# One dense step moved within each cycle of attention scores: from ahead of the last score to ahead of the third

## The chip, the cores and the metric

The kernel runs on one core of one Trainium2 chip. The metric is the device time of one execution in microseconds (us), lower is better. A core has five engines that work side by side: TensorE (PE in the profile; its weight loads are shown apart as PEld), VectorE (DVE), ScalarE (ACT), GpSimd (POOL) and SyncE (SP), which here issues most of the DMA transfers. PE writes its products to PSUM, a memory of eight banks, and ACT or DVE take them out.

## The reference

One transformer block over 2048 tokens of width 512, in f32: layer norm, attention with 32 heads of width 16 that share one key and one value head, residual, layer norm, gated feed-forward with a GELU gate and an inner width of 1792, residual.

```
def _A_ref(x, wq, wk, wv, wo):
    q = (x @ wq).reshape(B, S, H, Dh).transpose(0, 2, 1, 3)
    k = x @ wk
    v = x @ wv
    scores = jnp.einsum("bhqd,bkd->bhqk", q, k) * (Dh ** -0.5)
    p = _softmax(scores, axis=-1)
    o = jnp.einsum("bhqk,bkd->bhqd", p, v)
    return o.transpose(0, 2, 1, 3).reshape(B, S, H * Dh) @ wo

def _B_ref(x, w_gate, w_up, w_down):
    return (_gelu(x @ w_gate) * (x @ w_up)) @ w_down

x = A_x
h = x + _A_ref(_layernorm(x, axis=-1), A_wq, A_wk, A_wv, A_wo)
h2 = h + _B_ref(_layernorm(h, axis=-1), B_w_gate, B_w_up, B_w_down)
```

## The kernel before

**Attention.** The 2048 queries are cut into 4 blocks of 512, the 32 heads into 8 groups of 4, and the 2048 keys into 16 chunks of 128. For one block, one group and one chunk there are two *scores* in the sense of this document: `score(n)` (it calls `scores`, L368) issues two matmuls of PE side by side, for two heads, into a PSUM tile `s` of two banks, and one exponential of ACT (L372, 128 x 1024) that writes half of a tile `p`. An even and the next odd score fill one `p`. A *weighing* (`weigh`, L376) multiplies such a `p` by the values: four matmuls of 32 columns, which the profile shows as eight, into the accumulator `acc`. In the part of the program that matters there are two tiles `s`, so a score can be written only when the exponential of the score two before it has ended; there are five tiles `p`, and one `acc`, which DVE empties at the end of a group (L389).

**Dense work.** While the attention of block b runs, PE also does the dense work of block b - 1: the projection by `wo`, the layer norm's transposes, and the feed-forward. It is a generator (`dense`), and every `next` of it issues one *dense step*: two matmuls of 64 rows each, on the two halves of the array, into different banks (in `duo`, L548, and `weave`, L883). Three banks rotate among its products. A product is made in two halves: after the first half DVE marks the bank (L556, L906), and the other half of the array goes on with it at least LAG = 6 steps later; a bank is given to a new product at least 6 steps after its last one is done. DVE takes the finished products out (L744, L757 for gate and up, L825 for down), works on the GELU gate with ACT's tanh (L760), and also divides the attention's results (reciprocals, L416), for which it needs transfers by DMA.

**The order.** The order on PE, ACT, DVE, POOL and SP is written out by the program, instruction by instruction; nothing is moved by a scheduler. The 32 scores of a group and block are cut into six cycles of SIZES = (6, 5, 5, 6, 5, 5) scores, so that the cycles of a group begin with scores 0, 6, 11, 16, 22 and 27. A cycle issues its scores one by one, and after score j it issues as many dense steps as the j-th number of its `shares` says; at the end of the cycle come the weighings of all finished `p` but the newest. Which shares hold is set by the kind of the cycle: 8 cycles of a block are "long" (table LONG by the number of scores), 36 are "woven" (WOVEN, and LAST for the last cycle of a group), two are "short", one is a "gap" without dense steps of this kind, and the rest has none. In `(0, 5, 3, 3, 0)` no step follows the first score, 5 the second, 3 the third, 3 the fourth and none the fifth: the third score stands behind 5 dense steps. A step that ends a part of the dense work (CUT) ends the current share. Waiting work of DVE (`soon`, `lazy`) is taken from its list one entry for each score, so its place in DVE's order depends on where the scores stand among the steps; a product's evacuation and the load of later weights on SP (`done`, `next_w1`) stand at the step that ends it. Loads of queries (`load_q`, L353) for the next group are issued on SP at the third chunk of each group.

**Cycle names used below.** The fives that begin with scores 6 and 22 are *even fives*, the one that begins with 11 the *odd five*, the one that begins with 27 the *last five*.

Of the kernel before, what the change touches and what calls it, by code (L numbers as in the profile page):

```python
# [48 lines left out]
def kernel(  # L49
# [97 lines left out]
    def attend(first):  # L147
        with ExitStack() as outer:
            with tc.manual_schedule(
                engines={mybir.EngineType.PE, mybir.EngineType.Pool, mybir.EngineType.Activation}  # L150
            ):
                run(outer, first)


    def run(outer, first):
# [890 lines left out]
        width = 3  # L1046

        PLAIN = {5: (0,) * 5, 6: (0,) * 6}
        LONG = {5: (0, 5, 4, 3, 0), 6: (0, 5, 3, 3, 1, 0)}
        SHORT = {5: (0, 6, 3, 3, 0), 6: (0, 6, 3, 3, 0, 0)}  # L1050
        assert sum(SIZES) == 2 * KC
        assert [f for fs in RUNS for f in fs] == list(range(FC))
        assert [len(fs) for fs in RUNS] == [4] * (len(RUNS) - 1) + [2]

        WOVEN = {6: (0, 5, 3, 3, 3, 0), 5: (0, 5, 3, 3, 0)}
        LAST = (0, 5, 4, 3, 0)
        kinds = (
            ["long"] * 4 + ["gap"] + ["woven"] * 6 * len(SIZES) + ["long"] * 4 + ["short"] * 2
        )
# [5 lines left out]
        for c in range(LEAD[0], (NB - 1) * NG * len(SIZES)):  # L1065
# [10 lines left out]
            if kind == "long":  # L1076
                shares = LONG[size]
            elif kind == "woven":
                shares = LAST if cg == len(SIZES) - 1 else WOVEN[size]
            elif kind == "short":  # L1080
# [384 lines left out]
```

## Time and profile before

| | |
|---|---|
| median of 3 runs | 1422.04 us (1422.02 to 1422.42) |
| span of the profiled execution | 1421.8 us |
| PE busy | 1405.0 us, 99% |
| PEld busy | 760.5 us, 53% |
| ACT busy | 1036.2 us, 73% |
| DVE busy | 540.5 us, 38% |
| granted PE clock, mean | 0.999 |

The span runs from the first to the last instruction of one profiled execution; the times of the runs are taken without the profile. The ends of PE's matmuls are modelled and overlap the next ones, so a busy share of 99% does not tell that the matmuls follow each other without loss. The distances between starts do: they are read in the timeline, which lists instructions by start and length. A weight load row that is marked with a releaser stood waiting for it.

### The profile page before, as it was taken

The numbers are of one execution on the slowest core, as the hardware profiler recorded it, in microseconds if no ns is written. First come the engines' busy times: TensorE is split into PE (matmuls) and PEld (weight loads), VectorE is DVE, ScalarE is ACT, GpSimd is POOL, SyncE is SP. The second block draws the span as 40 slices with busy tenths as digits, with TensorE's granted clock in tenths as the row PEclk, the third lists the DMA queues.
The fourth block names the chain that finished last, engine by engine and source line by source line (L and its number), as shares of the span: only waits on it lengthen the run. The fifth ranks groups of instructions, "written<-read, shape, count | busy, mean of one in ns | idle before, by whom it ended". The sixth has DMA issues, their size and how long they took to land.

```text
span 1421.8 us, 25267 instructions
## 1 busy us (share of the span) xinstructions
PE 1405.0 (99%) x10502; PEld 760.5 (53%) x10502; DVE 540.5 (38%) x964; ACT 1036.2 (73%) x1149; POOL 229.3 (16%) x326
## 2 busy tenths in 40 slices
PE   9999999999999999999999999999999999999998
PEld 7533333225555555555555555554455555557886
DVE  7422322204352333514252432413343342427665
ACT  7699999997777787777777777877777777772000
POOL 6467776741000000000000000000000000002000
PEclk9999999999999999999999999999999999999999
DMA  4456766643242242213252332203243241434551
GB/s 158 155 187 213 228 202 220 204 162 107 82 157 82 88 143 86 88 41 113 94 168 78 100 132 84 89 23 123 92 140 116 86 145 35 140 125 137 178 207 63
DMA packets 66850, 180.31 MB, mean 127 GB/s; under 512 B 9484, under 2 KB 9484, under 8 KB 66696
## 3 DMA queue, kind: packets, MB, share of 16 engines
q1 hardware_dynamic: 56800, 144.43, 30.8%
q0 software_dynamic: 9760, 34.08, 7.4%
q8 instruction: 84, 1.38, 0.4%
q14 instruction: 38, 0.31, 0.1%
q10 hardware_dynamic: 168, 0.10, 0.0%
HBM read 130.87 MB, written 47.45 MB: 125 GB/s over the span
## 4 chain that ended last, share of the span: by engine, by line
PE 89%; ACT 6%; DVE 1%; DMA 1%; issue 1%; POOL 0%; SPq 0%; DVEq 0%; ACTq 0%; POOLq 0%
PE acc L376 31%; PE s L368 19%; PE pu L883 8%; PE pg L883 8%; ACT p L372 6%; PE pd L883 5%; PE pq L194 3%; PE pd L548 3%; PE pg L570 3%; PE pd L570 3%; PE pu L570 3%; PE pp L548 2%; PE pp L691 1%; PE pxt L623 1%; DMA w<-w_d 0%
## 5 line engine op out<-in xcount | busy, mean ns | idle before, releaser
L372 ACT ACTIVATE p<-s 128x1024 f32<-128x1024 f32 x1024 | 965.3, 1061 | 243.9 <-PE s L368 242.7
L376 PE MATMUL acc<-p,v_sb 128*32 128x512 f32 x4096 | 488.2, 598 | 0.1
L368 PE MATMUL s<-qg,kaug 50*128 50x512 f32 x1984 | 394.4, 432 | 4.1 <-ACT p L372 3.4
L368 PEld LDWEIGHTS s<-qg,kaug 50*128 50x128 f32 x1984 | 171.4, 184 | 284.3 <-ACT p L372 165.8
L376 PEld LDWEIGHTS acc<-p,v_sb 128*32 128x32 f32 x4096 | 109.4, 109 | 234.1 <-issue 225.8
L883 PE MATMUL pg<-x2h,w 64*128 64x512 f32 x672 | 211.9, 392 | 1.3 <-DMA w<-w_d 0.8
L883 PE MATMUL pu<-x2h,w 64*128 64x512 f32 x672 | 212.1, 392 | 0.0
L883 PEld LDWEIGHTS pg<-x2h,w 64*128 64x128 f32 x672 | 115.9, 186 | 14.3 <-DVE mark_pg L906 1.2
L883 PEld LDWEIGHTS pu<-x2h,w 64*128 64x128 f32 x672 | 116.0, 186 | 11.9
L883 PE MATMUL pu<-x2l,w 64*128 64x512 f32 x336 | 122.2, 391 | 0.0
L883 PE MATMUL pg<-x2l,w 64*128 64x512 f32 x336 | 122.1, 391 | 0.0
L126 POOL TENSOR_SCALAR rstd<-mv 128x1 f32<-128x1 f32 x16 | 3.5, 221 | 683.6 <-DVE mv L124 683.5
L760 ACT ACTIVATE ga<-ga 128x512 f32<-128x512 f32 x56 | 36.4, 656 | 88.7 <-DVE ga L755 88.7
L883 PE MATMUL pd<-w,gh 64*128 64x512 f32 x384 | 81.7, 391 | 0.0
L825 DVE TENSOR_TENSOR h<-h,pd 128x512 f32<-128x512 f32 x48 | 31.9, 684 | 114.7 <-PE pd L883 65.7
L389 DVE COPY oT<-acc 128x512 f32<-128x512 f32 x32 | 22.1, 691 | 138.5 <-PE acc L376 138.2
L1092 DVE SCALAR_TENSOR_TENSOR ga<-ga,g 128x512 f32<-128x512 f32 x72 | 49.7, 691 | 49.8 <-ACT ga L760 48.4
L416 DVE RECIPROCAL oc<-oc 128x128 f32<-128x128 f32 x64 | 56.3, 921 | 27.0 <-DMA oc<-acc_d 12.3
L744 DVE COPY g<-pg 128x512 f32<-128x512 f32 x56 | 38.7, 691 | 64.4 <-PE pg L883 58.7
L883 PEld LDWEIGHTS pu<-x2l,w 64*128 64x128 f32 x336 | 58.0, 186 | 6.8
L883 PEld LDWEIGHTS pg<-x2l,w 64*128 64x128 f32 x336 | 58.0, 186 | 5.2
L757 DVE TENSOR_TENSOR g<-g,pu 128x512 f32<-128x512 f32 x56 | 38.3, 683 | 40.5 <-PE pu L883 30.6
(260 smaller groups left out, 1406.3 us busy)
## 6 DMA issues: line engine op xcount, KB each, us to landing
w<-w_d SPq DMA_DIRECT2D x112, 512.0 KB
w<-w_d SPq DMA_DIRECT2D x28, 1024.0 KB
qg<-q_d SPq DMA_DIRECT2D x62, 200.0 KB
q_d<-qh SPq DMA_DIRECT2D x32, 256.0 KB
acc_d<-oT SPq DMA_DIRECT2D x31, 256.0 KB
oc<-acc_d SPq DMA_DIRECT2D x124, 64.0 KB
w_d<-w_0b POOLq DMA_DIRECT2D x14, 512.0 KB, 4.6
w_d<-w_1b POOLq DMA_DIRECT2D x14, 512.0 KB, 3.8
```

Of the source, the lines that this page charges most:

```text
L194: nc.tensor.matmul(pq, wt[:, d, c * P : (c + 1) * P], xt[:, d, :], start=(n == 0), stop=(n == 3 * DC - 1),)
L368: nc.tensor.matmul(s[:, a, :], kaug[rows, kc * P : (kc + 1) * P], qg[rows, u, :], start=True, stop=True,)
L372: nc.scalar.activation(p[:, 2 * u : 2 * u + 2, :], s, AF.Exp, scale=SCALE)
L376: nc.tensor.matmul(acc[32 * j : 32 * j + 32, :], v_sb[:, kc, :], p[:, j, :], start=(kc == 0), stop=(kc == KC - 1), skip_group_check=True,)
L416: nc.vector.reciprocal(oc[:, 1, sl], oc[:, 1, sl])
L548: nc.tensor.matmul(banks[k], lhsT[rows], rhs[rows], start=(turn == 0 and i == 0), stop=(turn == 1 and i == n - 1), skip_group_check=True,)
L570: nc.tensor.matmul(bank, lhsT, rhs, start=(i == 0), stop=(i == len(ts) - 1))
L744: nc.vector.tensor_copy(g, pg)
L757: nc.vector.tensor_tensor(g, g, pu, op=ALU.mult)
L760: nc.scalar.activation(a, a, AF.Tanh, scale=GELU_A * GELU_C)
L883: nc.tensor.matmul(e["bank"], lhsT[rows], rhs[rows], start=i == 0 and not e["both"], stop=last and e["both"], skip_group_check=True,)
L1092: (soon or lazy).pop(0)()
```

## The change

The number of dense steps in each cycle stays. In the tables LONG, WOVEN and LAST the share after the second score goes from 5 to 6, and the share ahead of the last score goes down by one (in the six-score long cycle the one ahead of the fifth score). SHORT and PLAIN stay, and so does every function.

```diff
-        LONG = {5: (0, 5, 4, 3, 0), 6: (0, 5, 3, 3, 1, 0)}
+        LONG = {5: (0, 6, 4, 2, 0), 6: (0, 6, 3, 2, 1, 0)}
         SHORT = {5: (0, 6, 3, 3, 0), 6: (0, 6, 3, 3, 0, 0)}
...
-        WOVEN = {6: (0, 5, 3, 3, 3, 0), 5: (0, 5, 3, 3, 0)}
-        LAST = (0, 5, 4, 3, 0)
+        WOVEN = {6: (0, 6, 3, 3, 2, 0), 5: (0, 6, 3, 2, 0)}
+        LAST = (0, 6, 4, 2, 0)
```

In the order of the instructions this moves, per cycle, the third score and those between it and the last one by one dense step each. On DVE a few entries of the waiting lists change places with marks and evacuations by one score. On SP, in two blocks, the two loads of queries of one group come behind one weight load instead of ahead of it. ACT's and POOL's orders stay.

## The prediction

> **What bounds the kernel now.** I read the page first, then the busy time of the stretch that the change touches, then who waits for whom in it, and last the timeline of single cycles. Columns of the stretch's row: sum, then busy time and instructions of PE, PEld, DVE, ACT and POOL, granted clock, DMA share, GB/s; of a timeline row: start, length (us), engine, line, operation, tiles, count, and in brackets the idle time before it with its releaser.
>
> ```profile
> span 1421.8 us, 25267 instructions
> PE 1405.0 (99%) x10502; PEld 760.5 (53%) x10502; DVE 540.5 (38%) x964; ACT 1036.2 (73%) x1149; POOL 229.3 (16%) x326
> 322.00:1280.00 958.00, 953.32 (x7844) 516.85 (x7848) 349.11 (x642) 731.18 (x795) 11.11 (x26) 1.00 0.31 102
> PEld s L368 <- ACT p L372: 75.9, 220, 1.2
> ACT p L372 <- PE s L368: 225.6, 147, 2.8
> ```
>
> All edited cycles lie between 322 and 1280 us. TensorE (PE) is busy for 953 of those 958 us at full granted clock, so time can only come from small hesitations inside its stream. The fourth row says where to look: the weight load (PEld) of a score stood waiting 220 times for an exponential of ScalarE (ACT). The fifth says that ACT in turn idles about once per cycle, waiting for a score. So the two engines hand over to each other within a cycle. Here is one woven cycle, five scores beginning with an even one, 3 weighings behind it:
>
> ```profile
> 496.29 0.39 PE L883 MATMUL pu<-x2l,w 64*128 64x512 f32 x1
> ...
> 496.52 0.40 PE L883 MATMUL pu<-x2h,w 64*128 64x512 f32 x1
> ...
> 496.70 0.19 PEld L368 LDWEIGHTS s<-qg,kaug 50*128 50x128 f32 x2 [0.22 <-ACT p L372]
> 496.76 0.45 PE L368 MATMUL s<-qg,kaug 50*128 50x512 f32 x2
> ...
> 497.04 0.40 PE L883 MATMUL pu<-x2h,w 64*128 64x512 f32 x1
> ...
> 498.45 0.39 PE L883 MATMUL pu<-x2h,w 64*128 64x512 f32 x1
> ...
> 498.53 0.19 PEld L368 LDWEIGHTS s<-qg,kaug 50*128 50x128 f32 x2
> ...
> 499.01 2.78 PE L376 MATMUL acc<-p,v_sb 128*32 128x512 f32 x24
> ```
>
> ACT in the same cycle, its first exponential and the third with the fourth:
>
> ```profile
> 495.62 1.03 ACT L372 ACTIVATE p<-s 128x1024 f32<-128x1024 f32 x1 [2.04 <-PE s L368]
> 497.44 1.95 ACT L372 ACTIVATE p<-s 128x1024 f32<-128x1024 f32 x2
> ```
>
> PE starts one slot (a dense step of two half-array matmuls, or a score of two) every 0.23 us: 496.29 to 496.52. There are two score buffers, so the third score needs the end of the first exponential: 495.62 + 1.03 = 496.65, and its load starts 0.05 later, at 496.70. That is 0.18 behind the start of the last dense step (496.52). The next dense step starts at 497.04, 0.52 after 496.52, where two slots take 0.46: 0.06 us are lost. So a load can be late by 0.18 - 0.06 = 0.12 us without cost; what goes beyond is paid in full. The last score's load is 0.08 late (498.53 against 498.45): free, with 0.04 to spare. ACT runs the exponentials of a cycle back to back, about 0.91 apart (495.62 to the third at 497.44).
>
> **The change, part by part.** No instruction is added or removed; the dense steps keep their order. In a cycle of kind long, woven or last, one dense step (two matmuls, 0.23 us) goes ahead of the third score and one fewer stands ahead of the last, or in the six-score long cycle ahead of the fifth. What this can win is the loss at the third score; what it can lose is lateness of a later one. With S the loss saved and d a delay of the exponential that the last score needs, the last load is late by (now) + S + d, because PE reaches it S earlier and ACT does not. A cycle therefore changes by -S + max(0, now + S + d - 0.12).
>
> The delay d is bounded so: the third score ends 0.23 later and its exponential may miss its turn. The lag from a score's end to its exponential, where ACT stands idle, is in the last cycle of a group:
>
> ```profile
> 382.20 0.39 PE L368 MATMUL s<-qg,kaug 50*128 50x512 f32 x2
> 382.70 1.03 ACT L372 ACTIVATE p<-s 128x1024 f32<-128x1024 f32 x1
> 383.62 1.02 ACT L372 ACTIVATE p<-s 128x1024 f32<-128x1024 f32 x1
> 383.46 0.64 PE L376 MATMUL acc<-p,v_sb 128*32 128x512 f32 x4
> ```
>
> Lag 382.70 - 382.59 = 0.11. The cycles, by type (each woven group of heads has two six-score cycles, two even fives, one odd five and one last five; 3 blocks of 6 groups):
>
> *Even fives, 36.* S = 0.06. The third score would end at 496.76 + 0.23 + 0.39 = 497.38, its exponential could start at 497.49 against 497.44 now: d = 0.05. Change -0.06 + (0.08 + 0.06 + 0.05 - 0.12) = +0.01, sum +0.4 us. If d were 0 it would be -0.04, sum -1.4.
>
> *Six-score cycles, 36.* The two kinds of them:
>
> ```profile
> 366.47 0.39 PE L883 MATMUL pg<-x2h,w 64*128 64x512 f32 x1
> ...
> 366.70 0.47 PE L368 MATMUL s<-qg,kaug 50*128 50x512 f32 x2
> 367.00 0.39 PE L883 MATMUL pg<-x2l,w 64*128 64x512 f32 x1
> 369.32 0.39 PE L883 MATMUL pu<-x2h,w 64*128 64x512 f32 x1
> 369.40 0.19 PEld L368 LDWEIGHTS s<-qg,kaug 50*128 50x128 f32 x2
> ```
>
> ```profile
> 387.67 0.39 PE L883 MATMUL pu<-x2l,w 64*128 64x512 f32 x1
> ...
> 387.89 0.48 PE L368 MATMUL s<-qg,kaug 50*128 50x512 f32 x2
> 388.21 0.40 PE L883 MATMUL pu<-x2h,w 64*128 64x512 f32 x1
> 388.62 1.95 ACT L372 ACTIVATE p<-s 128x1024 f32<-128x1024 f32 x2
> 390.55 0.39 PE L883 MATMUL pg<-x2l,w 64*128 64x512 f32 x1
> ...
> 390.62 0.19 PEld L368 LDWEIGHTS s<-qg,kaug 50*128 50x128 f32 x2
> ```
>
> In the first S = 367.00 - 366.47 - 0.46 = 0.07 and the last load is 0.08 late. In the second S = 388.21 - 387.67 - 0.46 = 0.08 and it is 0.07 late; the third score would end at 387.89 + 0.23 + 0.39 = 388.51, plus 0.11 is 388.62, exactly when its exponential starts now: d = 0, which I take for the first too. Changes -0.07 + 0.03 = -0.04 and -0.08 + 0.03 = -0.05, 18 each: -0.7 and -0.9 us. With d = 0.05 they are +0.01 and 0.
>
> *Odd fives, 18.* Nothing to save:
>
> ```profile
> 483.10 0.39 PE L883 MATMUL pg<-x2l,w 64*128 64x512 f32 x1
> 483.22 0.19 PEld L368 LDWEIGHTS s<-qg,kaug 50*128 50x128 f32 x2 [0.16 <-ACT p L372]
> 483.56 0.39 PE L883 MATMUL pg<-x2h,w 64*128 64x512 f32 x1
> ```
>
> The load is just 0.12 late and two slots take 0.46. I book 0.
>
> *Last fives (18) and five-score long cycles (17).* With 6, 4, 2 the fourth score comes 0.23 later and its exponential with it (ACT waits for it, as at 382.70), so the fifth ends near 383.62 + 0.23 + 1.02 = 384.9. Of the weighings behind it only the third reads it, and that starts two thirds of the 2.78 us for three (the row at 499.01), 1.8, after 383.46, at 385.3: 0.4 of cover; without it the 0.23 would be paid, 4 us in all. About five long ones begin even and save 0.05: -0.2 us.
>
> *Six-score long cycles, 7.* Their last score stands behind one dense step and waits openly for ACT already:
>
> ```profile
> 612.88 0.39 PE L548 MATMUL pd<-w,gl 64*128 64x512 f32 x2
> 613.41 0.19 PEld L368 LDWEIGHTS s<-qg,kaug 50*128 50x128 f32 x2 [0.57 <-ACT p L372]
> ```
>
> ACT's chain ends these cycles, so they save nothing and lose d, I take 0.03: +0.2 us.
>
> *VectorE and the queues.* Some DVE operations change places by one score, and in two of the three blocks one load of queries is issued behind one weight load instead of ahead of it on SP. The query loads:
>
> ```profile
> 798.44 1.77 SPq L528 DMA_DIRECT2D w<-w_d  x1
> 800.25 0.76 SPq L353 DMA_DIRECT2D qg<-q_d  x2
> ...
> 839.81 0.75 SPq L353 DMA_DIRECT2D qg<-q_d  x2
> ```
>
> They are issued a group (40 us) apart, early in one group for the next, so an exchange with an issue of 1.8 us has more than 30 us of cover; without it the next group's first score would be late by those 1.8. I book 0 for both; where DVE can bite is the third rival.
>
> **Sum**: +0.4 - 0.7 - 0.9 + 0 - 0.2 + 0.2 = -1.2 us. With d = 0 at the even fives -3.0; with d = 0.05 everywhere +0.6. The profiled execution spans 1421.8 us and would span 1420.6; the median of the runs lies 0.24 above that span, so 1420.8, between 1419.0 and 1422.6.
>
> **The rivals.** *First: the whole loss at the third score is won.* For it: no row shows a score ahead of a weighing with a load between 0.12 and 0.3 late, so the limit there is carried over from dense steps. The saving would be 36 x 0.06 + 18 x 0.07 + 18 x 0.08 + 0.2 = 5.1 us, 1416.9 us. Against: the 0.12 measured at 496.52, and a weighing needs the score's matmuls gone just as much. Beside this stands a rule of the Trainium skill (TensorE: Matmul & The Clock Gate, "Architectural detail: the array is 16× 32×32, not 1× 128×128"): a matmul can begin before its weight load completes. By that rule the lateness of the last score would be free up to its matmul; the row at 496.70, whose load was late by 0.18 and still cost 0.06, does not agree ahead of a dense step.
>
> *Second, slower: ACT runs dry and the last score pays.* If the third exponential starts 0.10 later instead of 0 to 0.05, every last load passes 0.12: even fives +0.06, sixes +0.06 and +0.05, odd fives 0.08 + 0.10 - 0.12 = +0.06 (their last load taken as late as the others'), in all 2.2 + 1.1 + 0.9 + 1.1 = 5.3 us, about 1427.3. It decides from d of some 0.04 on. For it: the third exponential already starts only 0.05 before its input would be there. Against: the lag of 0.11 is measured, and 0.10 more is not in any row.
>
> *Third: a dense bank comes free too late.* Three banks rotate among the dense products, and a run of six steps has no score inside it to give DVE time. It happens now where DVE waits for a transfer:
>
> ```profile
> DVE oc L416 <- DMA oc<-acc_d: 12.3, 7, 4.1
> 477.76 0.18 PEld L883 LDWEIGHTS pg<-x2h,w 64*128 64x128 f32 x1 [0.71 <-DVE h L825]
> ```
>
> At each of these seven places one slot less of cover costs up to 0.23, together 1.6: 1420.8 + 1.6 = 1422.4. Against: the order of the evacuations against the steps stays, and only the scores between them shift.
>
> **How the numbers follow.** The forecast has 0.62, the first rival 0.16, the second 0.12, the third 0.10. A measurement of this kernel can tell about 0.2% (2.8 us) from no change. Faster by more: the first rival and 0.02 of the forecast's tail, 0.18. Slower by more: the second rival and 0.01 of the third, 0.13. Within: 0.69. The range reaches from 1417.4, near the first rival, to 1424.4, half way into the second.
>
> **What would show it.** Right: third-score loads wait no more in the even fives and sixes (0.46 from the last step before it to the next one), last loads 0.14 to 0.19 late with the weighing 0.58 to 0.63 behind the last step instead of 0.56, cycles shorter by 0.05 at most, and the waits of scores for ACT moved and not gone. The first rival would show last loads as late with weighings still at 0.56; the second, third exponentials starting 0.10 behind their turn; the third, waits of dense loads for DVE beyond those of now. The forecast is wrong if a cycle's end moves by more than 0.06 either way.

## The result and the profile after

| | before | after |
|---|---|---|
| median of 21 runs each | 1422.04 us (1421.18 to 1423.15) | 1419.77 us (1418.94 to 1421.44) |
| span of the profiled execution | 1421.8 us | 1417.5 us |
| its own time | not measured | 1419.23 us |
| PEld of scores: idle | 284.3 us | 256.4 us |

The change makes the kernel 2.27 us faster: ratio 0.9984, with a 95% interval of 0.9977 to 0.9990, that is 1.4 to 3.3 us. That is real but below the 0.2% that the prediction set as the limit of "no change". The profiled span fell by more, 4.3 us, and a section below says why that pair shows too much.

First the head of the page of the changed kernel, then its busy time in the same stretch (columns as in the prediction), then its waits there: waiter, releaser, total, count, longest.

```profile
span 1417.5 us, 25266 instructions
PE 1401.8 (99%) x10502; PEld 786.5 (55%) x10502; DVE 542.6 (38%) x964; ACT 1041.4 (73%) x1149; POOL 228.7 (16%) x326
```

```profile
322.00:1280.00 958.00, 954.32 (x7873) 544.28 (x7874) 350.51 (x643) 738.63 (x798) 14.14 (x29) 1.00 0.30 103
```

```profile
ACT p L372 <- PE s L368: 215.7, 172, 2.8
PEld s L368 <- ACT p L372: 70.1, 157, 1.2
DVE oc L416 <- DMA oc<-acc_d: 11.3, 7, 3.4
```

PE is as "busy" as before, 954 of 958 us, and runs 29 more matmuls in the same stretch: the same work, packed closer. The waits of score loads for an exponential went from 220 with 75.9 us to 157 with 70.1 us. They have moved more than gone: 63 fewer, but the ones left are longer. A single cycle shows where. This is the even five that corresponds to the one in the prediction, from the timeline of the changed kernel (start, length, engine, line, operation, tiles, count, idle before with its releaser):

```profile
495.40 0.39 PE L883 MATMUL pg<-x2h,w 64*128 64x512 f32 x1
495.40 0.19 PEld L368 LDWEIGHTS s<-qg,kaug 50*128 50x128 f32 x2
495.63 0.39 PE L368 MATMUL s<-qg,kaug 50*128 50x512 f32 x2
...
495.87 0.39 PE L883 MATMUL pg<-x2l,w 64*128 64x512 f32 x1
...
497.03 0.39 PE L883 MATMUL pg<-x2h,w 64*128 64x512 f32 x1
497.21 0.19 PEld L368 LDWEIGHTS s<-qg,kaug 50*128 50x128 f32 x2 [0.22 <-ACT p L372]
497.25 0.46 PE L368 MATMUL s<-qg,kaug 50*128 50x512 f32 x2
497.64 0.64 PE L376 MATMUL acc<-p,v_sb 128*32 128x512 f32 x4
```

The load of the third score (495.40) starts with the last dense step before it, waits for nothing, and the next dense step follows 0.47 behind (495.40 to 495.87): before it was 0.52. The load of the last score (497.21) is now the one that waits for ACT; it is 0.18 late against the step at 497.03, and the weighing starts 0.61 behind that step (497.64). ACT runs the five exponentials without a pause, as before:

```profile
494.28 4.71 ACT L372 ACTIVATE p<-s 128x1024 f32<-128x1024 f32 x5 [1.95 <-PE s L368]
```

In the six-score cycle that answers to the second one of the prediction the last load is 0.17 late (390.55 to 390.72), and the weighing again 0.61 behind the step:

```profile
388.00 0.39 PE L883 MATMUL pg<-x2h,w 64*128 64x512 f32 x1
...
388.46 0.39 PE L883 MATMUL pu<-x2h,w 64*128 64x512 f32 x2
...
390.55 0.39 PE L883 MATMUL pg<-x2l,w 64*128 64x512 f32 x1
...
390.72 0.19 PEld L368 LDWEIGHTS s<-qg,kaug 50*128 50x128 f32 x2 [0.21 <-ACT p L372]
...
391.16 0.64 PE L376 MATMUL acc<-p,v_sb 128*32 128x512 f32 x4
```

**All cycles.** The next table takes the distance between the first scores of successive cycles, read from the starts in the two traces and grouped by the exact order of scores, steps and weighings; the medians leave the few disturbed cycles out. "Third" and "last" are the distances across that score: from the dense step ahead of it to the dense step or weighing behind it. Counts are below the plan's where a cycle is cut otherwise or a record is missing.

| cycle (number) | cycle, before to after | third | last | change x number |
|---|---|---|---|---|
| even fives (33) | 6.699 to 6.674 | 0.527 to 0.469 | 0.562 to 0.612 | -0.8 |
| odd fives (17) | 5.779 to 5.781 | 0.467 to 0.468 | 0.559 to 0.563 | 0 |
| sixes, two weighings (16) | 6.798 to 6.742 | 0.547 to 0.468 | 0.560 to 0.608 | -0.9 |
| sixes, three weighings (18) | 7.625 to 7.586 (13) and 7.594 (5) | 0.530 to 0.468 | 0.558 to 0.584 | -0.7 |
| last and long fives (27) | 6.876 to 6.862 | 0.474 to 0.468 | 0.562 to 0.565 | -0.4 |
| the same, two weighings (5) | 6.025 to 5.995 | 0.474 to 0.466 | 0.562 to 0.560 | -0.2 |
| long sixes (5) | 7.576 to 7.583 | 0.520 to 0.467 | 0.967 to 1.000 | 0 |

Added up before rounding, that is -2.8 us. The rest of the 4.3 us between the two spans is something else: single cycles in which a dense step, or a score, waited longer than in the others of their shape. Of the kernel before, from the view of waits:

```profile
PEld pg L883 <- DVE mark_pg L906: 1.2, 1, 1.2
PE pg L883 <- DMA w<-w_d: 0.8, 1, 0.8
PEld pg L883 <- DVE h L825: 0.7, 1, 0.7
PEld pg L883 <- DVE g L757: 0.7, 2, 0.5
```

The changed kernel's profile has none of these rows. Cycles longer than the median of their shape by over 0.1 us add up to 2.2 us in the profiled execution before (at 393.0, 474.3, 1016.1 and 1125.2 us) and to 0.4 after (1013.5 and 1122.3). They are called *bank waits* below, though not all of them wait for a bank. Those at 393.0 and 474.3 wait for DVE (the rows of L757 and L825). Those at 1013.5 and 1016.1 come from scores that wait for an exponential (0.28 us at the load at 1019.78 before and at 1017.28 after). The largest, 1.06 us in the cycle at 1125.2, waits for a transfer of weights; the rows of this place, before and after:

```profile
1123.14 0.37 SPq L528 DMA_DIRECT2D w<-w_d  x1
1128.59 0.16 DVE L906 COPY mark_pg<-pg 128x1 f32<-128x1 f32 x1 [1.23 <-PE pg L883]
1129.33 0.18 PEld L883 LDWEIGHTS pg<-x2h,w 64*128 64x128 f32 x1 [1.20 <-DVE mark_pg L906]
1129.36 0.46 PE L883 MATMUL pg<-x2h,w 64*128 64x512 f32 x1 [0.80 <-DMA w<-w_d]
```

```profile
1120.31 0.37 SPq L528 DMA_DIRECT2D w<-w_d  x1
1125.43 0.16 DVE L906 COPY mark_pg<-pg 128x1 f32<-128x1 f32 x1 [0.95 <-PE pg L883]
1125.48 0.18 PEld L883 LDWEIGHTS pg<-x2h,w 64*128 64x128 f32 x1 [0.30 <-issue]
```

The row at 1129.33 names DVE's mark, but the mark had ended at 1128.75, 0.58 earlier, and in the changed kernel the load starts ahead of its mark's end (1125.48 against 1125.59). What both loads follow, by 0.10 to 0.11 us, is the last of the 16 updates of the weight transfer's semaphore: at 1129.23 before, 6.1 us behind the issue, and at 1125.38 after, 5.1 us behind it. Both kernels issue this transfer 4.1 us behind the first exponential of the group, so the new order does not bring it earlier; why its last part took longer in one execution was not tested.

The profiled execution before took longer than the median of its runs (about 1423.5 us, by the link at the end of the account below) and the one after less (1419.23), so most of these 1.8 us belongs to the two executions and not to the pair. Without it the spans differ by 2.5 us, near the 2.27 of the medians; the 0.3 us between this and the sum over the cycles lies outside the table.

### The profile page after: what moved, and what is told of

It is laid out like the page before. It is cut to its first block, busy times and chain, and to the rows that moved or that the text cites. A ratio compares the mean times of both kernels' runs of the same rounds, so it can differ in the third digit from the quotient of the medians.

```text
span 1417.5 us, 25266 instructions
## 1 busy us (share of the span) xinstructions
PE 1401.8 (99%) x10502; PEld 786.5 (55%) x10502; DVE 542.6 (38%) x964; ACT 1041.4 (73%) x1149; POOL 228.7 (16%) x326
## 4 chain that ended last, share of the span: by engine, by line
PE 91%; ACT 6%; DMA 1%; issue 1%; DVE 0%; POOL 0%; SPq 0%; ACTq 0%; DVEq 0%; POOLq 0%
PE acc L376 31%; PE s L368 20%; PE pu L883 10%; PE pg L883 8%; ACT p L372 6%; PE pd L883 4%; PE pq L194 3%; PE pd L548 3%; PE pg L570 3%; PE pd L570 3%; PE pu L570 3%; PE pp L548 2%; DMA x<-in_A_x_dram 1%; PE pp L691 1%; PE pxt L623 1%
## 5 line engine op out<-in xcount | busy, mean ns | idle before, releaser
L368 PEld LDWEIGHTS s<-qg,kaug 50*128 50x128 f32 x1984 | 175.1, 184 | 256.4 <-ACT p L372 160.0
L825 DVE TENSOR_TENSOR h<-h,pd 128x512 f32<-128x512 f32 x48 | 31.9, 685 | 115.2 <-PE pd L883 66.3
L416 DVE RECIPROCAL oc<-oc 128x128 f32<-128x128 f32 x64 | 56.3, 921 | 30.1 <-DMA oc<-acc_d 11.3
L757 DVE TENSOR_TENSOR g<-g,pu 128x512 f32<-128x512 f32 x56 | 38.3, 683 | 40.1 <-PE pu L883 30.2
```

Source lines behind the costliest of these rows:

```text
L368: nc.tensor.matmul(s[:, a, :], kaug[rows, kc * P : (kc + 1) * P], qg[rows, u, :], start=True, stop=True,)
L416: nc.vector.reciprocal(oc[:, 1, sl], oc[:, 1, sl])
L757: nc.vector.tensor_tensor(g, g, pu, op=ALU.mult)
```

## The experiments

Four questions: which edit brings the time (one kind of cycle at a time), whether the limit of 0.12 us for a late load holds ahead of a weighing (more and fewer steps at the end), whether it is ACT's handover that the step is traded against (take ACT's wait away), and what the bank waits have to do with it. All times are medians of the kernel's runs; a ratio is against runs of the kernel before on the same chip, whose medians lay between 1421.99 and 1422.83, so kernels are best compared by their ratios. There are 21 runs of the kernels before and after, two of e4_seven, five and six of the pair with half exponentials, and 7 to 11 of the others.

| run | time, us | ratio (95%) | even five | sixes, two / three weighings |
|---|---|---|---|---|
| before | 1422.04 | | 6.699 | 6.798 / 7.625 |
| after | 1419.77 | 0.9984 (0.9977 to 0.9990) | 6.674 | 6.742 / 7.586 |
| e1_six | 1420.77 | 0.9991 (0.9982 to 1.0000) | 6.699 | 6.756 / 7.584 |
| e2_five | 1422.19 | 1.0002 (0.9993 to 1.0011) | 6.676 | 6.786 / 7.633 |
| e3_longlast | 1422.42 | 1.0002 (0.9993 to 1.0011) | as before | as before |
| e4_seven | 1444.23 | 1.0150 (1.0132 to 1.0169) | 6.909 | 6.976 / 7.823 |
| e5_late | 1421.86 | 0.9997 (0.9988 to 1.0006) | 6.691 | 6.738 / 7.590 |
| e6_early | 1421.04 | 0.9987 (0.9978 to 0.9996) | 6.691 | 6.762 / 7.608 |
| e7_half_before | 1417.74 | 0.9965 (0.9951 to 0.9978) | 6.629 | 6.702 / 7.562 |
| e8_half_after | 1418.17 | 0.9967 (0.9955 to 0.9979) | 6.627 | 6.698 / 7.553 |
| e9_spread | 1418.53 | 0.9976 (0.9966 to 0.9986) | 6.664 (51 cycles, the last fives among them) | 6.949 (15 steps) / 7.579 |
| e10_late_before | 1421.90 | 0.9996 (0.9987 to 1.0005) | 6.696 | 6.801 / 7.634 |
| e11_late_after | 1420.55 | 0.9983 (0.9974 to 0.9992) | 6.691 | 6.736 / 7.585 |
| e12_spread_late | 1418.53 | 0.9970 (0.9959 to 0.9981) | 6.664 (the same 51) | 6.929 (15 steps) / 7.585 |

### One kind of cycle at a time

e1_six changes the sixes of the woven part only, e2_five only its fives (even and odd), e3_longlast only the long cycles and the last fives; against the kernel before:

```diff
 # e1_six
-        WOVEN = {6: (0, 5, 3, 3, 3, 0), 5: (0, 5, 3, 3, 0)}
+        WOVEN = {6: (0, 6, 3, 3, 2, 0), 5: (0, 5, 3, 3, 0)}
 # e2_five
+        WOVEN = {6: (0, 5, 3, 3, 3, 0), 5: (0, 6, 3, 2, 0)}
 # e3_longlast
-        LONG = {5: (0, 5, 4, 3, 0), 6: (0, 5, 3, 3, 1, 0)}
+        LONG = {5: (0, 6, 4, 2, 0), 6: (0, 6, 3, 2, 1, 0)}
-        LAST = (0, 5, 4, 3, 0)
+        LAST = (0, 6, 4, 2, 0)
```

> Only the woven six-score cycles get the new shares (0, 6, 3, 3, 2, 0); fives, last and long cycles keep the old ones. Theory (handover): the loss at the third score goes and most of it comes back as lateness of the last score, so sixes with 2 weighings fall from 6.80 to 6.745 us and those with 3 from 7.63 to 7.59, together 36 cycles and -1.6 us (1420.4, ratio 0.9989); even fives stay at 6.70. Rival (the gain of the change comes from VectorE's and the queues' new order, which frees dense banks earlier, not from the scores): the sixes' cycle lengths stay and the time moves with the bank waits alone, 1422.0 or anything within a us of it.

> Only the woven fives get the new shares (0, 6, 3, 2, 0). Theory (handover): even fives fall from 6.70 to 6.675 (36 cycles, -0.9 us), odd fives stay at 5.78, sixes stay at 6.80 and 7.63; 1421.1, ratio 0.9994. By the term of the prediction for the even fives (+0.01 each) it would be 1422.4. Rival (banks and VectorE's order): cycle lengths without a bank wait stay, and only cycles with such a wait change, up to 2 us in all.

> Only the long cycles and the last cycle of each group get the new shares. Theory (handover): the last and the five-score long cycles have slack and fall by 0.01 to 0.02 each (6.88 to 6.865; 35 cycles, -0.5 us), the six-score long ones rise by 0.015 to 0.03 (7 cycles, +0.2 us): 1421.7, ratio 0.9998. Rival (the step taken from ahead of the last score is paid there): +0.05 on each last cycle, +0.9 us.

The cycles did what each edit says, and the kinds in the table that it leaves alone moved by 0.012 at most: in e1_six the sixes shrink and the even fives stay at 6.699, in e2_five the even fives shrink to 6.676 and the sixes stay, in e3_longlast the last and long fives go to 6.864. The totals show this for the sixes alone, and there just so (-1.2 us between the medians, with an interval that ends at 1.0000). e2_five, at 1422.19, lies nearer to the 1422.4 of the prediction's own term than to the 1421.1 expected from its cycles, and the three medians together move by -0.6 us where the whole change moves by -2.27. e2_five and e3_longlast came out 0.7 to 0.8 us above what their cycles add up to; their intervals reach 0.9 per mille (1.3 us) to either side, and their profiled executions hold 1.1 and 1.2 us of bank waits. A kind that is worth 0.8 us or less can be seen in the cycles, not in the total; that the three parts add up to the whole is shown for the cycles alone.

### A second step moved

```diff
 # e4_seven, against the kernel before
-        LONG = {5: (0, 5, 4, 3, 0), 6: (0, 5, 3, 3, 1, 0)}
+        LONG = {5: (0, 7, 4, 1, 0), 6: (0, 7, 3, 1, 1, 0)}
...
-        WOVEN = {6: (0, 5, 3, 3, 3, 0), 5: (0, 5, 3, 3, 0)}
-        LAST = (0, 5, 4, 3, 0)
+        WOVEN = {6: (0, 7, 3, 3, 1, 0), 5: (0, 7, 3, 1, 0)}
+        LAST = (0, 7, 4, 1, 0)
```

> One more step the same way as the change: 7 ahead of the third score and one fewer ahead of the last, fives (0, 7, 3, 1, 0), woven sixes (0, 7, 3, 3, 1, 0), last and long fives (0, 7, 4, 1, 0), long sixes (0, 7, 3, 1, 1, 0). Theory (handover): the third score has long been free at 6, but its exponential now starts 0.23 later and every later one with it, so the last score of each cycle, reached after as many steps as before, waits 0.2 to 0.23 longer: even fives 6.89, odd fives 5.98, sixes 6.97 and 7.81, last fives 6.88; 23 us slower than the changed kernel, 1442. Rival (a score only has to stand behind the exponential of two scores before it, more distance is free): no change, 1420.

1444.23 us (two runs), 1.5% slower: the handover theory holds to 2.2 us and to 0.02 us a cycle. An even five, from the timeline:

```profile
439.40 0.39 PE L883 MATMUL pd<-w,gh 64*128 64x512 f32 x1
439.81 0.19 PEld L368 LDWEIGHTS s<-qg,kaug 50*128 50x128 f32 x2 [0.45 <-ACT p L372]
439.81 0.50 PE L368 MATMUL s<-qg,kaug 50*128 50x512 f32 x2
440.24 0.64 PE L376 MATMUL acc<-p,v_sb 128*32 128x512 f32 x4
```

The third score had nothing left to give, so the step that leaves the end is paid in full: the last load is 0.41 late and the weighing 0.84 behind the step, 0.28 more than the 0.56 of an unhurried one (0.41 - 0.12 = 0.29).

### The step taken from another place

In the cycles of six and five of the woven part, e5_late leaves one step ahead of the last score and gives the freed one to the share before, and e6_early takes the step from the share behind the third score instead of the last one; both against the changed kernel:

```diff
-        WOVEN = {6: (0, 6, 3, 3, 2, 0), 5: (0, 6, 3, 2, 0)}
 # e5_late
+        WOVEN = {6: (0, 6, 3, 4, 1, 0), 5: (0, 6, 4, 1, 0)}
 # e6_early
+        WOVEN = {6: (0, 6, 3, 2, 3, 0), 5: (0, 6, 2, 3, 0)}
```

> The changed kernel with one more step moved in the woven cycles: fives (0, 6, 4, 1, 0), sixes (0, 6, 3, 4, 1, 0). Only the score before the last comes 0.23 later; the third and the last stay. Theory (handover: the last score waits for the exponential of the score two before it, and for nothing else): cycles as in the changed kernel, even fives 6.67, odd fives 5.78, sixes 6.74 and 7.59; 1419.8. Rival (what counts is how many steps separate the last two scores, since ScalarE then has less time): each of 90 cycles loses up to 0.23, 20 us, 1440.

> The changed kernel with the step given back ahead of the last score and taken from ahead of the one before it: fives (0, 6, 2, 3, 0), sixes (0, 6, 3, 2, 3, 0). Theory (handover): the hesitation moves again, to the score before the last, which now stands 0.23 earlier and waits: the weight load of the fourth score of an even five 0.17 to 0.19 late, 0.05 to 0.07 lost there, and the last score's load then on time; cycle lengths within 0.015 of the changed kernel's (6.67; sixes 6.74 and 7.59), 1419.8 in all. Rival (the last score's lateness was the only loss left, and three steps ahead of it cure it): even fives 6.63, sixes 6.69 and 7.56, 1417.0.

In e5_late the cycles are those of the changed kernel within 0.02 us: what counts is how many steps stand ahead of the last score in all, not which share they are in. The fourth exponential of an even five does start later (2.976 us behind the first, in the changed kernel 2.775), but the last score waits for the third one, which stays (1.869 against 1.852). (The ratio is 0.0013, or 1.8 us, above the changed kernel's; the cycles account for 0.5 of that. Its profile holds 1.6 us of bank waits, 1.1 of them at the weight transfer, which landed 5.8 us behind its issue; whether all its runs do is not known, and the rest stays open.) In e6_early the wait sits at the fourth score:

```profile
436.00 0.39 PE L883 MATMUL pg<-x2l,w 64*128 64x512 f32 x1
436.19 0.19 PEld L368 LDWEIGHTS s<-qg,kaug 50*128 50x128 f32 x2 [0.23 <-ACT p L372]
436.23 0.46 PE L368 MATMUL s<-qg,kaug 50*128 50x512 f32 x2
...
436.53 0.40 PE L883 MATMUL pg<-x2h,w 64*128 64x512 f32 x1
```

The load is 0.19 late and the next step 0.53 behind the last one, where 0.46 would be free: 0.07 lost. Over all even fives the median across the fourth score is 0.505 and across the last 0.577 (from 0.468 and 0.562 before the change). The rival that the loss at the third score could be won whole, at 1417.0, falls here too: at each of the places tried, the score behind the place that the step is taken from pays.

### ACT's wait taken away

From the first long cycle on, the exponential takes only half the columns, and GpSimd fills the other half of `p` with ones; so half of the exponentials are left out. e7_half_before does this in the kernel before, e8_half_after in the changed one. All lines behind it move by 8.

```diff
-            nc.scalar.activation(p[:, 2 * u : 2 * u + 2, :], s, AF.Exp, scale=SCALE)
+            if width == 3:
+                half = slice(0, T // 2)
+                if u == 0:
+                    nc.gpsimd.memset(p[:, :, T // 2 :], 1.0)
+                nc.scalar.activation(
+                    p[:, 2 * u : 2 * u + 2, half], s[:, :, half], AF.Exp, scale=SCALE
+                )
+            else:
+                nc.scalar.activation(p[:, 2 * u : 2 * u + 2, :], s, AF.Exp, scale=SCALE)
```

> The kernel before, but from the woven part on the exponential computes only 256 of its 512 columns per head (ScalarE 0.5 us instead of 0.91 per score); GpSimd fills the other half of p with ones, so the attention of those queries is left out. Theory (handover): no score waits any more; all cycles of one shape have one length, even and odd fives the same less their weighings, the third score's next step 0.23 behind it. Even fives 6.70 - 0.065 = 6.63, sixes 6.71 and 7.56, six-score long cycles 7.57 - 0.41 = 7.16; with the stretches that are now bound by ScalarE faster too, some 1405 us. Rival: the 0.30 behind the third score is no wait for ScalarE and stays.

> The same halved exponential in the changed kernel. Theory (handover): with nothing to wait for, the place of the step is worth nothing: the same time as the kernel before with halved exponentials within 0.7 us, and the same cycle lengths (6.63, 6.71, 7.56). Rival (the gain of the change comes from VectorE's, the banks' or the queues' order): it stays 2 us faster than its counterpart.

With ACT out of the way the position of the step is worth nothing: even fives 6.629 and 6.627, odd ones 5.781 and 5.769, sixes 6.702 and 6.698 or 7.562 and 7.553. The ratios, 0.9965 and 0.9967, are the same within their intervals, but these reach nearly 2 us to either side; it is the cycles, equal within 0.012 us, that test the theory: in the cycle the change acts on the handover between PE and ACT and on nothing else of that size. Waits of e7_half_before in the stretch, and one of its third scores:

```profile
PEld s L368 <- ACT p L376: 8.8, 11, 1.7
```

```profile
500.00 0.39 PE L891 MATMUL pg<-x2h,w 64*128 64x512 f32 x1
500.05 0.19 PEld L368 LDWEIGHTS s<-qg,kaug 50*128 50x128 f32 x2
500.23 0.40 PE L368 MATMUL s<-qg,kaug 50*128 50x512 f32 x2
...
500.46 0.40 PE L891 MATMUL pg<-x2h,w 64*128 64x512 f32 x1
```

Eleven waits where there were 220, and 0.46 across the third score. The level was a miss: 1405 us was expected and 1417.74 measured. The cycles that ACT still bounds lie mostly ahead of the edited part, and at the transitions between blocks GpSimd's fills, which wait for a `p` to be read, held the scores up (one such cycle took 10.95 us instead of 5.28). So the pair tells the difference, not what ACT costs in all.

### The remaining loss spread

After the change the sixes with two weighings pay 0.048 us at their last score, and the last fives of a group, whose third share of four puts the fourth score late, gain little. e9_spread gives the first cycle of each group, a six, one step more (15) and its last five one fewer (11); against the changed kernel:

```diff
-        LAST = (0, 6, 4, 2, 0)
+        LAST = (0, 6, 3, 2, 0)
...
-                shares = LAST if cg == len(SIZES) - 1 else WOVEN[size]
+                shares = LAST if cg == len(SIZES) - 1 else (0, 6, 3, 3, 3, 0) if cg == 0 else WOVEN[size]
```

> The changed kernel with one more dense step in the first cycle of each group, (0, 6, 3, 3, 3, 0), and one fewer in its last cycle, (0, 6, 3, 2, 0); the sum per group stays 73. Theory (handover): the last score of the first cycle comes 0.23 later and its load is late no more, so that cycle is 6.92 instead of 6.745 + 0.23 = 6.975; the last cycle of a group becomes an odd five, whose last load just fits, and falls by the whole 0.23 to 6.635. Gain 0.05 x 18 = 0.9 us over the changed kernel: 1418.9, ratio to before 0.9978. Rival (ScalarE late in the last cycle, with the fourth exponential ending behind): the last cycle falls by 0.1 only, and the sum is 1.5 us slower than the changed kernel.

1418.53 us (1418.35 to 1419.50), 1.2 us below the changed kernel (1.1 by the ratios), and clearly faster than the kernel before; the intervals of its ratio and of the changed kernel's overlap, so a gain over that one is likely, not shown. The first six with 15 steps takes 6.949: one step more than the 6.742 of the changed kernel, 0.207 for a step of 0.23. The last fives, one step shorter, have become even fives; taken alone they are 6.62 long, where those of the changed kernel are 6.855, so about 0.03 us is won in each group, some 0.5 us in all. The rest of the 1.2 us is not accounted for by these two kinds of cycle. A last five of a group, in its timeline:

```profile
382.80 0.39 PE L883 MATMUL pg<-x2l,w 64*128 64x512 f32 x1
...
382.92 0.18 PEld L368 LDWEIGHTS s<-qg,kaug 50*128 50x128 f32 x2 [0.16 <-ACT p L372]
383.02 0.40 PE L368 MATMUL s<-qg,kaug 50*128 50x512 f32 x2
...
383.35 0.64 PE L376 MATMUL acc<-p,v_sb 128*32 128x512 f32 x4
```

Its last load waits, is just 0.12 late, and the weighing stands at 0.55: free, with nothing to spare.

### The bank waits

In the prediction's third rival DVE marks or empties a dense bank late because its reciprocal (L416) stands waiting for a transfer. e10_late_before and e11_late_after put the reciprocals one cycle later in the kernel before and in the changed one, except in the last group of a block; e12_spread_late does it in e9_spread.

```diff
-                outs.extend([[] for _ in range(4 if b == 0 else 1)])
+                outs.extend([[] for _ in range(4 if b == 0 else 1 if g == NG - 1 else 2)])
```

> The kernel before, but the reciprocals of VectorE come one cycle (6 to 8 us) later after the end of a group than they do, except for the last group of a block, so that the transfers they read have landed. Theory: VectorE waits for transfers less than 2 us in all in place of 12 to 15, and the two to four cycles with a bank wait of 0.3 to 1.1 us are gone; cycle medians stay (6.70, 6.80, 7.63). 1421.3, runs within 1 us of each other. Rival (bank waits come from the dense work's own evacuations): they stay.

> The changed kernel with the same delay of the reciprocals. Theory (handover alone is the gain of the change): 2.3 us below its counterpart, as the two measured kernels are, with cycle medians of 6.67, 6.74 and 7.59: 1419.0, runs within 1 us. Rival (a good part of the gain is that the change happened to meet fewer bank waits): the difference to its counterpart falls to 1 us or less.

> The kernel with 15 steps in the first cycle of each group and 11 in the last, together with the delay of the reciprocals: 1418.2, 3.8 us below before, if both gains are of different places and add.

The transfers are no longer waited for. The waits of e10_late_before in the stretch:

```profile
DVE oc L416 <- DMA oc<-acc_d: 1.9, 2, 1.0
...
PEld pg L883 <- DVE mark_pg L906: 0.6, 1, 0.6
```

12.3 us of DVE's waiting became 1.9. The bank waits shrank in this profile from 2.2 us to 0.6, but did not go, and the time did not move (ratio 0.9996, interval 0.9987 to 1.0005). Those at about 1013 and 1123 us come back in nearly every profile, in e12_spread_late with 1.4 us.

The place at 1123 us is one that these edits do not reach. In ten of the 14 profiles, e10_late_before, e11_late_after and e12_spread_late among them, the load of weights there starts 0.10 to 0.11 us behind the last update of its own weight transfer, which came 4.8 to 6.3 us behind the issue. The row of `mark_pg` above is such a case: the transfer's last update is at 1127.89, the load at 1127.99. In the other four (e2_five, e3_longlast and both kernels with half exponentials) the load starts 0.05 us behind DVE's product at L757 (there moved to L765), which stood behind a reciprocal. So the third rival's cause is real, and a late weight transfer stands beside it.

With the reciprocals later in both, the change still brings 1.35 us (1421.90 to 1420.55; between the fastest runs, 1421.80 to 1419.87, 1.9), where the theory expected 2.3 and the rival 1 or less; the cycles of the two differ by 1.7 us in all. So most of the gain does not come from bank waits. e12_spread_late lies at 0.9970 and e9_spread at 0.9976, with intervals that overlap, so that both gains add is not shown.

## Why the prediction was right, and where it was off

The forecast was 1420.8, 1.2 us below the median; 1419.77 came, 2.3 below, in the range and on the side named. The mechanism is the one forecast; that the total came so near is in part luck, as one kind of cycle was booked with the wrong sign, and e5_late, whose cycles are those of the changed kernel within 0.02 us, has a ratio of 0.9997. By its own steps:

- **What bounds the kernel** held. e7_half_before and e8_half_after show it by an edit: without waits for ACT in the cycles the move changes nothing.
- **The limit of 0.12 us, carried over from a dense step to a weighing** held; this was the open link, and the first rival (1416.9) was its failure. In the changed kernel the weighing stands 0.56 behind the last step for loads up to 0.12 late, 0.583 at 0.14, 0.598 at 0.16, 0.607 at 0.17, 0.633 at 0.20 and 0.783 at 0.34. Beyond 0.13 the cost rises one for one.
- **The rule of the Trainium skill** by which that rival would have had its way (TensorE: Matmul & The Clock Gate, "Architectural detail: the array is 16× 32×32, not 1× 128×128"): a matmul beginning ahead of the end of its load did not save a late load here. The matmul at 497.25 does begin ahead of the end of its load (497.21 + 0.19), as the page has it, and yet the cost is there; the same rows speak against the rival, 0.41 late costing 0.28 in e4_seven most plainly.
- **Six-score cycles**: -0.04 and -0.05 each were booked, -1.6 us; -0.031 to -0.056 were measured, -1.6 us.
- **Even fives: the term that was mis-sized.** +0.01 each was booked, -0.025 measured: -0.8 us for 33 of them instead of +0.4 for 36, which is most of what the forecast missed. Its saving S was right (0.058 for 0.06). The delay d was too big: over all even fives the third exponential starts 1.825 us behind the first before and 1.852 after, d = 0.027, where 0.05 was worked out from rounded rows of a single cycle. The formula with the measured d gives 0.08 + 0.058 + 0.027 - 0.12 = 0.045 at the last score; 0.050 was measured. The other 0.017 has no term in it: third and last score together give 0.058 - 0.050 = 0.008, and the rest lies between dense steps, some of which follow by 0.227 instead of 0.233. It comes back in e2_five (6.676), while the odd fives do not have it, and in e5_late and e6_early it is absent. It is absent in e11_late_after too (6.691), which has the changed kernel's order on PE, so that order alone does not make it. What does was not tested.
- **Odd fives** at 0: measured +0.002.
- **Last and long fives**: -0.2 us booked, -0.5 measured. No 0.23 was paid for the fourth score that comes later: the cover of 0.4 from the weighings held. The 0.014 saved in each of 27 was not booked; 0.006 of it is at the third score.
- **Long sixes**: +0.03 booked for each, +0.007 measured, 0.52 to 0.47 at the third score against 0.04 and 0.03 lost at the two behind it.
- **The second rival, ACT dry (1427.3)**: it needed d of 0.10 in all; the even fives have 0.027, and ACT's row of five exponentials grew from 4.69 to 4.71.
- **The third rival, banks late (1422.4)**: bank waits exist in both profiles, and are less after, not more. The largest of them is a wait for a transfer of weights, for which the prediction has no term.
- **The link from the span to the median was wrong.** The prediction took the median 0.24 above the profiled span. All 13 profiled executions since have their own time beside the span and lie 1.7 to 1.8 above it. The span of 1421.8 thus belongs to an execution of about 1423.5 us, above all 21 runs of the kernel before, and it holds 2.2 us of bank waits. The difference that was added to it was worked out from cycles, so the forecast suffered little; a sum made against that span's true relation would have come out the same, as a change against the median.

Of the list of what would show it right, the third score at 0.46 to 0.47, last loads 0.14 to 0.19 late with weighings at 0.58 to 0.63, and waits that moved all came. "Cycles shorter by 0.05 at most" came to 0.056 in one kind.

## What to carry to other kernels

Where two engines hand over to each other through two buffers, take the distance from start to start across each handover, not the busy share or the sum of idle time: PE was 99% busy before and after, and 70 of 76 us of its waits for ACT were still there when the gain was in. A wait costs only what exceeds the slack in front of it (0.12 us here), so work is best placed so that each handover is late by just that slack; moving one step more (e4_seven) cost ten times what the first had won. A releaser that the profile names has to be checked by its end: the mark named at 1129.33 had been done for 0.58 us, and the transfer behind it shows only in the row of the matmul. An effect of 0.2% needs single cycles to be told from scatter, and a delay booked as a term is better taken as the median over all cycles than from one.

## What was not expected of the hardware

- The price of a late weight load has a sharp corner at 0.12 to 0.13 us and is the same ahead of a dense step of 64 rows and ahead of a weighing of 128 rows by 32 columns.
- An exponential starts 0.10 us behind the end of an even score but 0.04 behind that of an odd one, where ACT stands idle for both. The trace has ends of matmuls modelled, and what makes the difference was not looked into.
- The last of the 16 updates of a weight transfer can come long behind the others: in the profile before 15 were there by 1126.62 and the last came at 1129.23, with PE waiting; in the changed kernel's the last two came at 1123.91 and 1125.38.
- The device time lies 1.7 to 1.8 us above the profiled span in all 13 kernels, whether the span is 1416.0 or 1443.2 us.
